# A one-core adaLN block whose 2,121 operations run in a written-out order: another order past the first 140

## The chip, the core and the metric

The kernel runs on one core of a Trainium2 chip. The time is the device time of one execution in microseconds. The core has a matrix engine (TensorE, called PE in the profile; its weight loads are PEld), a vector engine (VectorE, DVE), an activation engine (ScalarE, ACT), a general engine (GpSimd, POOL) and SyncE (SP), which here only issues DMAs. Each engine works off its own instruction list in the order in which the program wrote it, and waits on semaphores that the others raise.

## What is computed

One transformer block with modulation, in bfloat16, on 2048 rows of 640:

```python
mod = (silu(c) @ w_mod).reshape(1, 6, 1, 640)         # sa, ca, ga, sb, cb, gb
h = layernorm(x) * (1 + ca) + sa
q, k, v = split_heads(h @ wqkv)                        # 32 heads of 20
s = q @ k.T * 20 ** -0.5                               # key j is seen by query i if 0 <= i - j < 256
x = x + ga * ((softmax(s) @ v) @ wo)
h = layernorm(x) * (1 + cb) + sb
x = x + gb * ((sigmoid(h @ w_gate) * (h @ w_up)) @ w_down)   # hidden width 1536
```

## The kernel before

**The tiling.** The 2048 rows are cut into eight chunks of 256. A chunk goes through layer norm (`ln1`), the projection to q, k and v (`qkv`), windowed attention (`attention`), the output projection with the residual (`outproj`) and the gated MLP (`mlp`). Chunk a attends to itself and to chunk a-1. All weights stay in SBUF once they are loaded.

**Score groups and bursts.** For each chunk and each half of its heads, attention runs five score groups (three in chunk 0): four "main" ones and one "edge" one, built by `score_set`. All groups write one PSUM tile `S`, which has a single buffer. ACT takes the exponentials out of it into an `E` tile: a main group by one activation of 512 columns and one of 1536, an edge group by four of 512 columns (line 1015). POOL then zeroes what lies outside the window with affine selects (`masks`, line 1040): "far" and "near" over 512 columns, "diag" over 1024. When the four `E` tiles of a half are masked, PE multiplies them by V in one run of matmuls, here called a burst; from chunk 1 on it is issued in front of the second score group of the following half. Each half gives one burst, sixteen in all.

**The other work.** Between score groups PE runs chains of the projections, of `wo` and of the MLP. They write the PSUM tile `M`, which has four buffers; ACT or DVE must empty a buffer before the next chain can use it. ACT applies the tanh from which the sigmoid is made (line 1209), DVE the product with the "up" half (`hh`, line 1211). The gate `gb` is folded into `w_down`: twelve multiplications `wd<-wd,gbc` (line 1192), for which a row `gbc` has to come back from DRAM. The modulation by scale and shift (lines 811 and 812), five column blocks a chunk, and most evacuations of PSUM (lines 893 and 894) may run on ACT, DVE or POOL.

**The order of the work.** `op` records each operation with the engines that can do it. The list `PRIO` (line 342) has one number per recorded operation. `schedule` (line 152) sorts all operations by it; the number modulo 5 names the engine. So `PRIO` fixes each engine's instruction list completely. While it walks through the sorted list, `schedule` also keeps a reckoning of when each operation starts and ends, and uses that for one thing that ends up in the program: where a tile's pool has several buffers, it gives the new tile the buffer that comes free first. `emit` then writes the engines' lists, with a semaphore wait where a producer is on another engine or a buffer has an earlier user. DMAs take 24 semaphores in turn.

Of the kernel before, what the change touches and what calls it, by code (L numbers as in the profile page):

```python
# [25 lines left out]
SWITCH = 0.095  # L26
ENGATTR = {"pe": "tensor", "act": "scalar", "dve": "vector", "pool": "gpsimd", "sp": "sync"}
ENGS = ("pe", "act", "dve", "pool", "sp")
OVERLAP = {"pe": 0.0, "act": 0.085, "dve": 0.075, "pool": 0.045, "sp": 0.0}
# [52 lines left out]
class Prog:  # L82
# [69 lines left out]
    def schedule(self):  # L152


        free = {e: START for e in ENGS}
        bw = 0.0
        lastturn = False
        order = {e: [] for e in ENGS}
        dmacnt = [0] * NDMA
        dmalast = [None] * NDMA  # L160
        rr = 0
        pemode = 0
        portend = 0.0
        freed = {}

        def slot_time(pool, s):
            ten = pool.tenant[s]
            if ten is None:
                if not all(x.done for x in pool.init[s]):
                    return None  # L170
                return max([x.end + x.lat for x in pool.init[s]], default=0.0)
            return None if ten.left else freed[ten]

        def take(t, s):
            ten = t.pool.tenant[s]
            t.prev = list(t.pool.init[s]) if ten is None else list(ten.rel)
            t.slot = s
            t.pool.tenant[s] = t

        for o in sorted(self.ops, key=lambda x: x.prio):  # L180
            assert all(d.done for d in o.deps), o.tag
            e = ENGS[o.prio % 5]
            assert e in o.engs, (o.tag, e)
            o.eng = e
            st = max([o.tmin, free[e] + (SWITCH if e == "pe" and o.mode != pemode else 0.0)]
                     + [d.end + (0.0 if d.eng == "pe" and e == "pe" else d.lat) for d in o.deps])
            if o.isdma and e == "sp":
                st = max(st, bw - QMAX)
            for t in o.tiles:
                if t.slot is None:  # L190
                    step = 1 if t.mate is None else 2
                    best = None
                    for s in range(0, len(t.pool.tenant), step):
                        rts = [slot_time(t.pool, s + k) for k in range(step)]
                        if None not in rts and (best is None or max(rts) < best[0]):
                            best = (max(rts), s)
                    assert best is not None, (o.tag, t.name)
                    if t.mate is None:
                        take(t, best[1])
                    else:  # L200
                        take(t, best[1] + t.odd)
                        take(t.mate, best[1] + 1 - t.odd)
                for x in t.prev:
                    st = max(st, x.end + x.lat)
            if e == "dve" and o.port:
                st = max(st, free["pool"])
            elif e == "pool":
                st = max(st, portend)
            o.start = st
            if e == "pe":  # L210
                pemode = o.mout
            dur = o.dur[e]
            free[e] = st + dur - OVERLAP[e]
            if e == "dve" and o.port:
                portend = free[e]
            if o.isdma:
                turn = o.dlat > 3.0
                if e == "sp" and bw - st > 2.0:
                    free[e] += 0.35 if o.dur[e] > 1.0 else 0.1
                bw = max(st + o.dlat, bw + (MIXED if turn != lastturn and bw > st + o.dlat else 0.0)) + o.work  # L220
                lastturn = turn
                o.end = max(bw - 0.83, st + dur)
                s = rr
                rr = (rr + 1) % NDMA
                dmacnt[s] += 16
                o.key, o.val = f"d{s}", dmacnt[s]
                if dmalast[s] is not None:
                    o.deps.append(dmalast[s])
                dmalast[s] = o
            else:  # L230
                o.end = st + dur
            order[e].append(o)
            o.done = True
            for t in o.tiles:
                t.left -= 1
                if t.left == 0:
                    last = {}
                    for x in t.ops:
                        if x.isdma:
                            last[x] = x  # L240
                    for e2 in ENGS:
                        xs = [x for x in t.ops if x.eng == e2 and not x.isdma]
                        if xs:
                            last[e2] = max(xs, key=lambda x: x.start)
                    t.rel = list(last.values())
                    freed[t] = max(x.end + x.lat for x in t.rel)
        self.order = order
        self.span = max(o.end for o in self.ops)
# [88 lines left out]
def c_pe(n):  # L337
# [3 lines left out]
PE_EPS = 0.14  # L341
PRIO = [
# [124 lines left out]
START = 0.8  # L467
PORTLAG = 0.05
MIXED = 0.55
# [837 lines left out]
```

## Time and profile before

| what | value |
|---|---|
| median of 3 runs | 325.99 us (325.92, 325.99 and one of 528.63) |
| span of the profiled execution, first to last instruction | 324.3 us |
| instructions | 11,594 |
| PE busy | 317.3 us |
| ACT, DVE, POOL busy | 212.3, 211.8, 187.2 us |
| DMA | 37.85 MB |

The execution that was profiled is listed by its span alone; the median of the runs lies 1.7 us above that span. The third run, far above the others, says nothing about the kernel. A busy PE means that at least one matmul was in flight: a matmul of 256 columns is shown with 273 ns, while in a chain the next one starts after 0.109 us.

### The profile page before, as it was taken

The numbers are of one execution on the slowest core, as the hardware profiler recorded it, in microseconds if no ns is written. First come the engines' busy times: TensorE is split into PE (matmuls) and PEld (weight loads), VectorE is DVE, ScalarE is ACT, GpSimd is POOL, SyncE is SP. The second block draws the span as 40 slices with busy tenths as digits, with TensorE's granted clock in tenths as the row PEclk, the third lists the DMA queues.
The fourth block names the chain that finished last, engine by engine and source line by source line (L and its number), as shares of the span: only waits on it lengthen the run. The fifth ranks groups of instructions, "written<-read, shape, count | busy, mean of one in ns | idle before, by whom it ended". The sixth has DMA issues, their size and how long they took to land.

```text
span 324.3 us, 11594 instructions
## 1 busy us (share of the span) xinstructions
PE 317.3 (98%) x4872; PEld 222.7 (69%) x4873; DVE 211.8 (65%) x424; ACT 212.3 (65%) x316; POOL 187.2 (58%) x276
## 2 busy tenths in 40 slices
PE   8999999989999999999999999999999999999997
PEld 3564545446776568765776467877786788787885
DVE  5797898778687959674477475837463769264332
ACT  1899985889876687788687867786767764011120
POOL 5128869976668694847585939382939691012100
DMA  7998799989891383824405394340213032202101
GB/s 249 371 333 299 165 269 180 200 137 183 260 164 22 83 109 77 152 61 101 85 22 82 97 103 110 92 69 5 81 40 88 3 79 53 76 20 64 40 2 40
DMA packets 71694, 37.85 MB, mean 117 GB/s; under 512 B 45274, under 2 KB 70362, under 8 KB 71642
## 3 DMA queue, kind: packets, MB, share of 16 engines
q1 hardware_dynamic: 69616, 35.31, 48.3%
q10 hardware_dynamic: 2026, 1.80, 2.1%
q8 instruction: 38, 0.62, 0.8%
q14 instruction: 14, 0.11, 0.1%
HBM read 21.30 MB, written 5.25 MB: 82 GB/s over the span
## 4 chain that ended last, share of the span: by engine, by line
PE 73%; DMA 2%; SPq 2%; DVE 1%; POOL 1%; issue 0%; DVEq 0%
PE M L668 61%; PE S L669 6%; PE M L669 5%; DMA gbc<-gate 2%; SPq L803 2%; DVE wd L1192 1%; POOL x L793 0%; POOL st L788 0%; DVE hh L1211 0%; POOL E L1040 0%; DVE x L1230 0%; DVEq L310 0%
## 5 line engine op out<-in xcount | busy, mean ns | idle before, releaser
L1040 POOL TENSOR_SCALAR_AFFINE_SELECT E<-E 128x512 bf16<-128x512 bf16 (+1 forms) x176 | 142.6, 836 | 68.7 <-ACT E L1015 67.0
L1015 ACT ACTIVATE E<-S 128x512 bf16<-128x512 f32 (+2 forms) x184 | 150.9, 878 | 47.4 <-PE S L669 46.5
L668 PE MATMUL M<-wqkv,hT 128*128 128x480 bf16 (+1 forms) x340 | 73.9, 355 | 0.6 <-ACT hT L846 0.5
L668 PE MATMUL M<-h2T,wu 128*128 128x256 bf16 x480 | 68.0, 273 | 0.5 <-DVE hh L1211 0.5
L668 PE MATMUL M<-h2T,wg 128*128 128x256 bf16 x480 | 67.8, 273 | 0.0
L668 PE MATMUL M<-wd,hh 128*128 128x320 bf16 (+2 forms) x396 | 58.1, 295 | 0.0
L1209 ACT ACTIVATE sig<-M 128x512 f32<-128x512 f32 x48 | 28.9, 602 | 44.1 <-PE M L668 41.7
L1211 DVE SCALAR_TENSOR_TENSOR hh<-sig,M 128x512 bf16<-128x512 f32 x48 | 32.4, 681 | 37.1 <-ACT sig L1209 24.0
L668 PEld LDWEIGHTS M<-h2T,wu 128*128 128x128 bf16 x480 | 45.9, 98 | 8.4 <-issue 1.2
L668 PEld LDWEIGHTS M<-h2T,wg 128*128 128x128 bf16 x480 | 45.7, 98 | 7.1
L668 PEld LDWEIGHTS M<-wqkv,hT 128*128 128x128 bf16 x340 | 30.1, 98 | 27.6 <-DMA wqkv<-in_A_wqkv_dram 1.6
L668 PEld LDWEIGHTS M<-wd,hh 128*128 128x128 bf16 x396 | 36.8, 98 | 14.3 <-DVE hh L1211 0.2
L669 PEld LDWEIGHTS S<-QT,KT 20*64 20x64 bf16 (+1 forms) x1856 | 19.9, 100 | 21.3 <-ACT E L1015 12.0
L1230 DVE TENSOR_TENSOR x<-M,x 128x320 bf16<-128x320 f32 (+2 forms) x33 | 15.6, 476 | 27.2 <-PE M L668 27.2
L669 PE MATMUL S<-QT,KT 20*64 20x256 bf16 (+5 forms) x1856 | 32.1, 228 | 1.2 <-ACT E L1015 1.2
L776 DVE BATCH_NORM_STATS2 st<-x 128x6 f32<-128x320 bf16 x64 | 28.6, 477 | 2.3 <-DMA x<-in_A_x_dram 1.9
L1082 DVE STREAM_TRANSPOSE T<-M 128x512 f32<-128x512 f32 x32 | 21.5, 698 | 9.2 <-PE S L669 8.0
L668 PE MATMUL M<-wo,oT 128*128 128x320 bf16 x160 | 25.4, 299 | 0.0
L669 PE MATMUL M<-E,V 128*32 128x128 bf16 (+1 forms) x960 | 22.8, 246 | 0.8 <-ACT E L1015 0.4
L781 POOL TENSOR_SCALAR st<-st 128x2 f32<-128x2 f32 x16 | 3.7, 234 | 33.8 <-DVE st L778 33.6
L669 PEld LDWEIGHTS M<-E,V 128*32 128x32 bf16 x960 | 19.2, 97 | 5.3 <-issue 2.9
L1091 DVE STREAM_TRANSPOSE On<-Tn 128x1024 bf16<-128x1024 bf16 x16 | 19.8, 1240 | 0.3
(77 smaller groups left out, 240.2 us busy)
## 6 DMA issues: line engine op xcount, KB each, us to landing
x<-in_A_x_dram SPq DMA_DIRECT2D x23, 160.0 KB, 2.3
doc<-On SPq DMA_DIRECT2D x56, 40.0 KB
wd<-in_B_w_down_dram SPq DMA_DIRECT2D x4, 480.0 KB
wd<-in_w_mod_dram SPq DMA_DIRECT2D x5, 320.0 KB
wqkv<-in_A_wqkv_dram SPq DMA_DIRECT2D x4, 400.0 KB
wu<-in_w_mod_dram SPq DMA_DIRECT2D x5, 320.0 KB
oT<-doc SPq DMA_DIRECT2D x8, 192.0 KB, 2.5
out_dram<-x SPq DMA_DIRECT2D x9, 160.0 KB
```

The lines of the kernel that those rows point to most:

```text
L668: return e.matmul(o, l, r, start=st, stop=sp, skip_group_check=True)
L669: return e.matmul(o, l, r, start=st, stop=sp, tile_position=tp, skip_group_check=True)
L776: A("dve", lambda e, g, bi=bi, j=j: e.bn_stats(v(bi * 12 + j * 6, 6), src[bi].ap[:, j * 320:(j + 1) * 320]), 0.48, reads=[src[bi].r()], wr ...
L781: A("pool", lambda e, g: e.tensor_scalar(v(28, n), var(), EPS, None, op0=ALU.add), 0.2, reads=[st.r(("m", bi)) for bi in range(n)], writes ...
L803: return e.dma_start_transpose(dst(), src())
L1015: A("act", lambda e, eng: e.activation(dst(), src(), ACT.Exp, scale=SM_SCALE), c_act(n), reads=[Sp.r()], writes=[E.r(key)], prio=3, tag=f" ...
L1040: A("pool", lambda e, eng: e.affine_select(rows(dst), rows(src), pattern=[[0, 8], [sign, n]], compare_op=ALU.is_ge, fill=0.0, base=base, c ...
L1082: A("dve", lambda e, g, h=h: e.transpose(T1.ap[:, 512 * h:512 * h + 512], X[h].ap), 0.694, reads=[X[h].r()], writes=[T1.r(h)], prio=3.5, t ...
L1091: A("dve", lambda e, g: e.transpose(On.ap[:], Tn.ap[:]), 1.22, reads=[Tn.r()], writes=[On.r()], prio=4, tag=f"tr2_{a}")
L1209: A("act", lambda e, g, pg=pg, sg=sg: e.activation(sg.ap[:], pg.ap[:], ACT.Tanh, scale=0.5), c_act(512), reads=[pg.r()], writes=[sg.r()], ...
L1211: A("dve", lambda e, g, pu=pu, sg=sg, f0=f0: e.scalar_tensor_tensor(out=hh.ap[:, f0:f0 + 2, :], in0=sg.ap[:].rearrange("p (a b) -> p a b", ...
L1230: A("dve", lambda e, g, ps=ps, bi=bi, c0=c0, n=n: e.tensor_tensor(x1[bi].ap[:, c0:c0 + n], ps.ap[:, 0:n], x1[bi].ap[:, c0:c0 + n], op=ALU. ...
```

## The change

`PRIO` gets other numbers. The first 140 operations in the sorted order stay the same operations in the same order. From there on the order is another, found by a search over draws of whole traces that began at an order with few priced moves. `schedule` no longer keeps its reckoning of time: the buffer of each tile is read from a new list `SLOTS` (709 tiles, numbered in order of first mention), and the constants of the reckoning go. 72 operations change engine:

| operation | moves |
|---|---|
| emptying PSUM of q, k, v (`evqk`, `evv`, `evqt`) | 17 from ACT to DVE, 13 from DVE to ACT |
| transposed x out of PSUM (`ahTe`) | 3 from DVE to ACT, 1 from ACT to DVE |
| modulation ahead of attention (`amodu`) | 3 POOL to ACT, 3 DVE to ACT, 2 ACT to DVE, 2 ACT to POOL |
| modulation ahead of the MLP (`bmodu`) | 7 POOL to ACT, 6 ACT to POOL, 5 DVE to ACT, 3 DVE to POOL, 2 ACT to DVE, 2 POOL to DVE |
| scaling `w_down` (`wds`) | 2 POOL to DVE, 1 DVE to POOL |

ACT then has 337 operations instead of 333, DVE 422 instead of 424, POOL 262 instead of 264; PE keeps 907 and SP 193. The arithmetic of every operation stays as it is.

```diff
-SWITCH = 0.095
-OVERLAP = {"pe": 0.0, "act": 0.085, "dve": 0.075, "pool": 0.045, "sp": 0.0}
...
     def schedule(self):
-        free = {e: START for e in ENGS}
...
+        tiles = {}
+        def number(t):
+            if t is not None and t not in tiles:
+                tiles[t] = len(tiles)
+                number(t.mate)
+        for o in self.ops:
+            for t in o.tiles:
+                number(t)
         for o in sorted(self.ops, key=lambda x: x.prio):
             e = ENGS[o.prio % 5]
             o.eng = e
-            st = max([o.tmin, free[e] + (SWITCH if e == "pe" and o.mode != pemode else 0.0)]
-                     + [d.end + (0.0 if d.eng == "pe" and e == "pe" else d.lat) for d in o.deps])
...
             for t in o.tiles:
                 if t.slot is None:
-                    best = None
-                    for s in range(0, len(t.pool.tenant), step):
-                        rts = [slot_time(t.pool, s + k) for k in range(step)]
...
+                    s = SLOTS[tiles[t]] if SLOTS else 0
+                    ten = t.pool.tenant[s]
+                    t.prev = list(t.pool.init[s]) if ten is None else list(ten.rel)
+                    t.slot = s
+                    t.pool.tenant[s] = t
...
 PRIO = [
-    23, 28, 258, 8, 43, 33, 958, 18, 1448, 38, 3, 507, 513, 72, 67, 48, 53, 58, 76, 84, 101, 99, 144, 149, 154, 159,
+    23, 28, 258, 8, 43, 33, 708, 18, 728, 38, 3, 507, 513, 72, 67, 48, 53, 58, 76, 84, 101, 99, 144, 149, 154, 159,
...
+SLOTS = [
+    0, 1, 3, 2, 0, 0, 0, 1, 0, 2, 0, 1, 3, 0, 1, 2, 3, 0, 0, 1, 0, 2, 0, 0, 3, 1, 0, 4, 5, 1, 3, 2, 2, 3, 2, 1, 3,
...
```

More of the change, by code (lines that the diff above doesn't have):

```diff
@@ L152, in schedule @@
     def schedule(self):
-        free = {e: START for e in ENGS}
-        bw = 0.0
-        lastturn = False
         order = {e: [] for e in ENGS}
@@ L161, in schedule @@
         rr = 0
[L162 to L178, printed above, removed]
+        tiles = {}
[6 more added lines that the diff above has]
+                number(t)
         for o in sorted(self.ops, key=lambda x: x.prio):
@@ L184, in schedule @@
             o.eng = e
-            st = max([o.tmin, free[e] + (SWITCH if e == "pe" and o.mode != pemode else 0.0)]
-                     + [d.end + (0.0 if d.eng == "pe" and e == "pe" else d.lat) for d in o.deps])
-            if o.isdma and e == "sp":
-                st = max(st, bw - QMAX)
             for t in o.tiles:
                 if t.slot is None:
-                    step = 1 if t.mate is None else 2
-                    best = None
-                    for s in range(0, len(t.pool.tenant), step):
-                        rts = [slot_time(t.pool, s + k) for k in range(step)]
[L195 to L215, printed above, removed]
-            if o.isdma:
[L217 to L223, printed above, removed]
-                rr = (rr + 1) % NDMA
[L225 to L231, printed above, removed]
+                    s = SLOTS[tiles[t]] if SLOTS else 0
@@ new lines, in schedule @@
+                    ten = t.pool.tenant[s]
+                    assert ten is not None or all(x.done for x in t.pool.init[s]), (o.tag, t.name)
+                    assert ten is None or ten.left == 0, (o.tag, t.name)
+                    t.prev = list(t.pool.init[s]) if ten is None else list(ten.rel)
+                    t.slot = s
+                    t.pool.tenant[s] = t
+            if o.isdma:
+                dmacnt[rr] += 16
+                o.key, o.val = f"d{rr}", dmacnt[rr]
+                if dmalast[rr] is not None:
+                    o.deps.append(dmalast[rr])
+                dmalast[rr] = o
+                rr = (rr + 1) % NDMA
@@ L237, in schedule @@
                     last = {}
[L238 to L244, printed above, removed]
+                    for x in sorted(t.ops, key=lambda x: x.prio):
+                        last[x if x.isdma else x.eng] = x
                     t.rel = list(last.values())
-                    freed[t] = max(x.end + x.lat for x in t.rel)
         self.order = order
-        self.span = max(o.end for o in self.ops)
     def emit(self):
@@ L338, in c_pe @@
     return max(n, 64) / 2400.0 + 0.0027
-PE_EPS = 0.14
 PRIO = [
[3 rows of a table removed]
[3 rows of a table added]
     92, 87, 187, 237, 242, 247, 253, 263, 272, 267, 280, 275, 290, 300, 305, 286, 317, 296, 322, 311, 376, 357, 386,
[1 row of a table removed]
[1 row of a table added]
     541, 495, 501, 665, 677, 480, 485, 491, 565, 570, 576, 545, 551, 630, 652, 525, 555, 561, 625, 660, 681, 685,
[111 rows of a table removed]
[111 rows of a table added]
+]
+SLOTS = [
[20 rows of a table added]
 ]
@@ L466 @@
 DSAFE = 1.5
-START = 0.8
-PORTLAG = 0.05
-MIXED = 0.55
 NPB = 0
@@ L484 @@
 WSE = (("dve", "pool"), ("dve", "pool"))
-QMAX = 4.5
 WDT = 72.0
```

247 rows, old and new, of tables (PRIO, SLOTS) are left out of this document.

## The prediction

> **What bounds the kernel now.** First the page's busy table, then the table by stage, which says where PE, the busiest engine, still waits.
>
> ```profile
> span 324.3 us, 11594 instructions
> PE 317.3 (98%) x4872; PEld 222.7 (69%) x4873; DVE 211.8 (65%) x424; ACT 212.3 (65%) x316; POOL 187.2 (58%) x276
> ...
> 0.00:12.00 12.00, 9.98 (x88) 5.07 (x90) 7.11 (x24) 4.38 (x10) 4.73 (x25) 1.00 0.86 286
> 12.00:55.00 43.00, 42.46 (x568) 23.54 (x569) 37.31 (x85) 37.08 (x62) 28.26 (x43) 1.00 0.94 261
> 55.00:70.00 15.00, 13.85 (x247) 7.38 (x239) 11.38 (x27) 12.13 (x18) 13.27 (x20) 1.00 1.06 186
> 70.00:90.00 20.00, 19.07 (x353) 14.10 (x356) 15.66 (x28) 16.88 (x28) 13.03 (x17) 1.00 0.93 212
> 90.00:150.00 60.00, 60.00 (x1029) 41.32 (x1018) 46.02 (x92) 43.59 (x62) 41.75 (x56) 1.00 0.51 92
> 150.00:210.00 60.00, 59.99 (x1088) 42.16 (x1087) 36.31 (x68) 46.02 (x67) 40.43 (x56) 1.00 0.47 87
> 210.00:270.00 60.00, 60.00 (x1081) 46.23 (x1079) 34.24 (x62) 43.70 (x61) 42.08 (x57) 1.00 0.24 54
> 270.00:324.30 54.30, 51.91 (x450) 42.88 (x446) 23.74 (x45) 8.47 (x15) 3.65 (x7) 1.00 0.14 40
> ```
>
> The columns are the stretch and its length, then busy time for PE, PEld, DVE, ACT and POOL, then granted clock and DMA. Length less PE busy is PE's idle time: 2.02 us to 12 us, then 0.54, 1.15 and 0.93 us up to 90 us, 0.01 us in the 180 us from 90 to 270, and 2.39 us at the end, where PE is done and the last rows go out. **PE bounds the kernel**, and after 90 us nothing keeps it waiting. The timeline of PE shows what is behind the idle time from 12 to 90 us.
>
> ```profile
> 38.23 0.84 PE L669 MATMUL M<-E,V 128*32 128x256 bf16 x32 [0.35 <-DVE hT L858]
> ...
> 48.66 0.43 PE L669 MATMUL S<-QT,KT 20*64 20x256 bf16 x24 [0.17 <-ACT E L1015]
> ...
> 61.60 0.43 PE L669 MATMUL S<-QT,KT 20*64 20x256 bf16 x24 [0.27 <-ACT E L1015]
> ...
> 64.13 0.43 PE L669 MATMUL S<-QT,KT 20*64 20x256 bf16 x24 [0.30 <-ACT E L1015]
> ...
> 67.91 0.43 PE L669 MATMUL S<-QT,KT 20*64 20x256 bf16 x24 [0.42 <-ACT E L1015]
> ...
> 70.48 1.50 PE L669 MATMUL M<-E,V 128*32 128x128 bf16 x64 [0.42 <-ACT E L1015]
> ...
> 86.54 1.25 PE L668 MATMUL M<-h2T,wu 128*128 128x256 bf16 x10 [0.51 <-DVE hh L1211]
> ...
> 295.58 6.68 PE L668 MATMUL M<-wd,hh 128*128 128x320 bf16 x48
> ```
>
> Seven waits make 2.44 of the 2.62 us. A busy PE isn't always PE at its peak: 48 matmuls of 320 columns in 6.68 us are some 0.136 us from start to start, but one is in flight for 0.30 us, so up to 0.16 us of each wait hides behind the matmul before it. Seven waits hide at most 1.1 us. What an order of the same work can still win is therefore about 2.62 + 1.1 = 3.7 us: it **cannot reach 322 us**. By 2%, about what a measurement of this kernel can tell from no change, faster means under 319.5 us.
>
> **The change part by part.** PE's 907 operations are the same, with the same columns: nothing is added to the bound. I followed the two lists through the recorded operations. SP's 193 DMAs keep their order exactly. PE keeps 624 of its 907 operations in a common order, ACT 226, DVE 258, POOL 156. The sum goes stage by stage, against the span of 324.3 us; the 1.7 us between it and the median of 325.99 are carried over.
>
> *Up to 12 us*: the first 140 operations stand as they were, 0 (±0.2).
>
> *12 to 55 us*: 0.54 us is idle. In front of the second burst ACT now has 48 operations instead of 51, three evacuations of PSUM fewer (one takes 0.58 us in the timeline of ACT below). The rows for what is weighed here and further on:
>
> ```profile
> L1015 ACT ACTIVATE E<-S 128x1536 bf16<-128x1536 f32 x56 | 81.1, 1449 | 17.5 <-PE S L669 17.3
> L1015 ACT ACTIVATE E<-S 128x512 bf16<-128x512 f32 x120 | 67.3, 602 | 29.4 <-PE S L669 29.0
> L811 ACT ACTIVATE hT<-hT,mA 128x256 bf16<-128x256 bf16 x14 | 7.8, 595 | 0.0
> L858 DVE TENSOR_SCALAR hT<-M,mA 128x256 bf16<-128x256 f32 x9 | 4.6, 537 | 0.1
> ```
>
> But the burst at 38.23 us waits for a DVE evacuation of 537 ns into whose `M` buffer it writes; in the new list a transpose and both buffers of the burst still follow such evacuations after 0.4 to 0.6 us of matmuls; those of the burst's own buffers have gone to ACT. The wait stays. I take -0.1, from -0.5 (all idle gone) to +0.5 (the wait twice).
>
> *55 to 70 us*: here ACT decides. Its timeline:
>
> ```profile
> 62.14 1.94 ACT L1015 ACTIVATE E<-S 128x512 bf16<-128x512 f32 x2 [0.59 <-PE S L669]
> 63.97 2.07 ACT L811 ACTIVATE hT<-hT,mA 128x256 bf16<-128x256 bf16 x4
> 65.93 1.92 ACT L1015 ACTIVATE E<-S 128x1536 bf16<-128x1536 f32 x2
> 67.74 0.58 ACT L893 ACTIVATE stg<-M 128x480 bf16<-128x480 f32 x1
> 68.44 1.94 ACT L1015 ACTIVATE E<-S 128x1536 bf16<-128x1536 f32 x2
> ```
>
> `S` has one buffer, so a score group waits for the exponentials of the one before. Four modulations stand together between two groups' exponentials: the group at 64.13 us is written by about 64.5, its exponentials begin only at 65.93, and the group at 67.91 waits for their end. The new list puts two of these modulations there and two one group later. A pair takes about 1.1 us, of which the writing of the group (0.43 us) and its two hand-overs cover the most. So the first pair saves up to 1.0 us at the first place and costs a few tenths at the second. Of 0.42 + 0.42 us at 67.91 and 70.48 I take half back: -0.4, from -0.8 to +0.4. POOL, busy for 13.27 of 15 us here, has the same total of work ahead of the burst at 70.48 in both lists, ACT 0.3 us more; hence the upper end.
>
> *70 to 90 us*: the wait of 0.51 us at 86.54 comes from DVE.
>
> ```profile
> 80.35 0.69 DVE L1211 SCALAR_TENSOR_TENSOR hh<-sig,M 128x512 bf16<-128x512 f32 x1 [0.94 <-ACT sig L1209]
> 83.16 2.65 DVE L1192 TENSOR_TENSOR wd<-wd,gbc 128x640 bf16<-128x640 bf16 x4 [2.12 <-DMA gbc<-gate]
> 85.72 1.27 DVE L1211 SCALAR_TENSOR_TENSOR hh<-sig,M 128x512 bf16<-128x512 f32 x2
> ...
> 73.62 4.26 SPq L803 DMA_TRANSPOSE KT<-stg  x1
> 77.92 0.58 SPq L570 DMA_DIRECT2D gbc<-gate  x1
> ```
>
> DVE stood 2.12 us at a `wd` multiplication whose `gbc` had not landed, and two finished halves of the MLP queued behind it with their `M` buffers full. `gbc` is issued at the same place of SP's list as before, so it lands no earlier. But the new DVE list has three `hh` operations ahead of the first `wd` multiplication instead of one, and then `wd` multiplications by ones, twos and fours between the others. The two `hh` that queued now go first. I take -0.5, from -0.7 to 0; what is late next is the fourth `hh`, behind three multiplications of some 0.55 us, by which time `gbc` is there.
>
> *90 to 270 us*: nothing can be won, so every difference costs. Three things feed PE here.
>
> ```profile
> L1040 POOL TENSOR_SCALAR_AFFINE_SELECT E<-E 128x512 bf16<-128x512 bf16 x112 | 75.8, 689 | 42.5 <-ACT E L1015 42.1
> L1040 POOL TENSOR_SCALAR_AFFINE_SELECT E<-E 128x1024 bf16<-128x1024 bf16 x64 | 69.3, 1093 | 26.2 <-ACT E L1015 24.9
> L1209 ACT ACTIVATE sig<-M 128x512 f32<-128x512 f32 x48 | 28.9, 602 | 44.1 <-PE M L668 41.7
> ```
>
> First the four `M` buffers. Of 290 reuses, 59 had under 1.3 us of matmuls between the last write of the old contents and the first of the new; now 79 have. The price of a tight one: at 38.23 us, 0.38 us of matmuls against an evacuation of 0.537 us cost 0.35 us, so the hand-over adds 0.19 us. A tanh then needs 0.602 + 0.19 = 0.79 us. Two reuses behind a tanh now have 0.70 us and lose 0.1 each; reuses of 0.68 us or more behind a residual (some 0.48 us on DVE) fit. But the engine must also be free at once, and there are 20 more places where it has to be. Second the masks: by the new order POOL has up to 1.5 us less and at most 0.2 us more ahead of the bursts after 130 us, so those come no later. Third ACT: by the eighth burst it has 2.7 us more ahead of it, but in 90 to 150 us ACT is busy for 43.59 of 60 us, so 16 us are free. I take +0.5, from 0 to +3.0 (each of the 20 new tight places losing 0.15 us).
>
> *From 270 us*: the last burst is followed by the same 182 operations of PE in both lists, ending with the same down-projection: 0, to +0.5.
>
> Sum: 0 - 0.1 - 0.4 - 0.5 + 0.5 + 0 = **-0.5 us**; span 323.8, time 325.5 us. The ends add up to -2.2 and +4.6.
>
> **The rivals.** *All waits go.* If stalls between 12 and 90 us vanish with their hidden part and nothing new comes, the time is 325.99 - 3.7 = 322.3, or 323 with a few tenths left. For it: both causes at 67.91 and 86.54 are taken apart. Against it: the wait at 38.23 is still in the list, and the buffers are tighter.
>
> *Buffers and masks come late, by little each time.* If the 20 tighter reuses lose 0.15 us each and the changed ACT order lets three or four bursts start 0.3 us later, +3.0 + 1.0 against the gains of 1.0 gives 329.0. For it: the 0.01 us idle in 180 us shows how exactly the old order fits the chip. Against it: ACT and POOL have a quarter of their time free there.
>
> *Slower by over 2%: a chunk's keys come late and PE cools.* One transposing DMA held SP for 4.26 us (73.62). SP's list is unchanged, but what it transposes is now written by operations that have moved. If one such hold is no longer covered, the score groups behind it, and all work that hangs on them, leave PE idle for 4.3 us. What a long pause then costs shows at the start:
>
> ```profile
> 1.31 2.74 PE L649 MATMUL S<-E 128*128 128x512 bf16 x6 [1.31 <-DVE E L644]
> ...
> 4.33 1.91 PE L649 MATMUL S<-E 128*128 128x512 bf16 x4
> ```
>
> Four matmuls of 512 columns take 1.91 us, the last 0.63 in flight, so some 0.43 us apart, where 0.136 x 512/320 = 0.22 would be full speed. This lasts from 1.31 to about 6 us and loses 2.4 us. Together with the gains not made: 326.0 + 4.3 + 2.4 = 332.7. It decides where a pause gets as long as that, and the longest after 12 us is 0.51 us now: little speaks for it. The Trainium skill, "TensorE: Matmul & The Clock Gate", Part 1, says that the array falls to half its clock after an idle window of about 3.4 us and needs about as much sustained work to come back; by that rule this rival's price is right and the other cases pay none of it. The slow matmuls at the start agree, although the clock column says 1.00 there; no trace here shows a pause of that length later.
>
> *The change does nothing that matters*: PE is bound from 90 us on, and if ACT's and DVE's regrouping is swallowed too, the time stays at 326.0.
>
> **How the numbers follow.** The forecast, 325.5, with its neighbourhood from 324.4 to 327.5 that also holds the last rival: 0.55. All waits go, 322.2 to 324.4: 0.22. Late by little, 327.5 to 332.5: 0.16. Over 332.5: 0.06. Under 319.5, against the bound: 0.01. So faster 0.01, slower 0.06, the same 0.93. The range goes from 323.0, which leaves about 0.08 below, to 329.5, which leaves 0.12 above.
>
> **What would show it.** Right: PE's idle time at 55 to 70 us under 1 us, none behind `hh` near 86 us, modulations on ACT in twos near 64 us, and 90 to 270 us idle for a few tenths. Wrong: PE idle behind tanh, residual or transposed evacuations after 90 us adding to over 2 us; bursts waiting for affine selects; or any PE pause over 2 us.

## The result and the profile after

The changed kernel takes **327.89 us** (median of six runs, 327.73 to 328.31) against 326.06 us for the kernel before beside it (five runs from 325.26 to 326.23, and the one of 528.63): a ratio of 1.0065, with a 95% interval from 1.0054 to 1.0076. By 2% that is no change, and the predicted range of 323.0 to 329.5 us holds it. But the forecast was half a microsecond faster, and the kernel is slower, by 1.8 us in the medians and 2.1 us by the ratio. The span of the profiled execution went from 324.3 to 326.2 us.

The head of the page and the table by stage of the changed kernel; the columns are those of the prediction, with the stretch from 90 us on cut at 110:

```profile
span 326.2 us, 11574 instructions
PE 316.9 (97%) x4872; PEld 221.8 (68%) x4873; DVE 211.8 (65%) x422; ACT 215.1 (66%) x320; POOL 184.8 (57%) x274
```

```profile
0.00:12.00 12.00, 8.96 (x83) 4.21 (x85) 6.70 (x23) 4.06 (x10) 4.71 (x25) 1.00 0.86 278
12.00:55.00 43.00, 42.19 (x561) 23.62 (x560) 39.10 (x89) 35.91 (x59) 27.33 (x43) 1.00 0.92 259
55.00:70.00 15.00, 13.97 (x249) 7.47 (x247) 8.99 (x21) 12.73 (x21) 13.12 (x19) 1.00 1.11 186
70.00:90.00 20.00, 19.16 (x331) 13.65 (x332) 16.05 (x28) 15.57 (x24) 15.13 (x21) 1.00 0.88 213
90.00:110.00 20.00, 18.87 (x332) 13.12 (x323) 18.44 (x38) 12.75 (x19) 12.04 (x17) 1.00 0.51 82
110.00:150.00 40.00, 40.00 (x722) 27.81 (x715) 26.73 (x49) 33.52 (x51) 26.49 (x37) 1.00 0.48 93
...
270.00:326.20 56.20, 53.76 (x515) 44.06 (x512) 24.39 (x45) 10.89 (x19) 3.38 (x7) 1.00 0.16 42
```

PE is busy for as long as before (316.9 against 317.3 us): the work is the same, the idle time grew. By stage, length less PE busy, before and after: to 12 us 2.02 and 3.04; 12 to 55 us 0.54 and 0.81; 55 to 70 us 1.15 and 1.03; 70 to 90 us 0.93 and 0.84; **90 to 110 us 0.00 and 1.13**; at the end 2.39 and 2.44; between 110 and 270 us 0.01 us at most in either. The first of these, up to 12 us, is put down to the execution and not to the change: the first 140 operations are the same, and what PE waits for there is weights from DRAM (0.52 and 0.56 us after, 0.19 us before). Executions of either kernel and of the experiments below have between 2.00 and 3.04 us there (the five built on the old order 2.24 on average, the seven built on the new one 2.56, and the two groups overlap); whether some of the 0.3 us between the averages belongs to the order is not settled. So idle time is compared from 12 to 110 us: **2.62 us before, 3.81 after**.

The waits of PE in the timeline of the changed kernel:

```profile
38.72 0.84 PE L635 MATMUL M<-E,V 128*32 128x256 bf16 x32 [0.17 <-POOL hT L778]
...
53.21 0.43 PE L635 MATMUL S<-QT,KT 20*64 20x256 bf16 x24 [0.52 <-ACT E L981]
...
64.92 0.43 PE L635 MATMUL S<-QT,KT 20*64 20x256 bf16 x24 [0.37 <-ACT E L981]
...
65.89 2.85 PE L634 MATMUL M<-wqkv,hT 128*128 128x480 bf16 x12 [0.55 <-ACT hT L777]
...
71.26 1.50 PE L635 MATMUL M<-E,V 128*32 128x128 bf16 x64 [0.42 <-ACT E L981]
...
89.52 1.50 PE L635 MATMUL M<-E,V 128*32 128x128 bf16 x64 [0.42 <-DVE hh L1177]
...
98.84 0.85 PE L634 MATMUL M<-wo,oT 128*128 128x320 bf16 x5 [1.13 <-DVE x L1130]
```

The new one is the last: the output projection needs an `M` buffer that DVE's residual addition has yet to empty. What DVE did ahead of it, from the timeline of DVE, and POOL's list over the same time:

```profile
86.54 1.76 DVE L1158 TENSOR_TENSOR wd<-wd,gbc 128x640 bf16<-128x640 bf16 x2
...
89.30 2.97 DVE L1158 TENSOR_TENSOR wd<-wd,gbc 128x640 bf16<-128x640 bf16 x4
...
95.71 1.38 DVE L1158 TENSOR_TENSOR wd<-wd,gbc 128x640 bf16<-128x640 bf16 x1
...
97.02 1.37 DVE L1158 TENSOR_TENSOR wd<-wd,gbc 128x640 bf16<-128x640 bf16 x1
...
98.31 1.07 DVE L1130 TENSOR_TENSOR x<-M,x 128x320 bf16<-128x320 f32 x2
```

```profile
95.35 1.40 POOL L1006 TENSOR_SCALAR_AFFINE_SELECT E<-E 128x1024 bf16<-128x1024 bf16 x1 [2.53 <-ACT E L981]
...
96.70 1.34 POOL L1006 TENSOR_SCALAR_AFFINE_SELECT E<-E 128x1024 bf16<-128x1024 bf16 x1
```

The two `wd` multiplications at 95.71 and 97.02 us last 1.38 and 1.37 us. The same instruction, over all ten of before and all eleven of after (shortest, median, longest, in ns):

```profile
L1192 DVE TENSOR_TENSOR wd<-wd,gbc x10: 468/484/866, 83.2 to 93.9; 128x640 bf16<-128x640 bf16 x10
```

```profile
L1158 DVE TENSOR_TENSOR wd<-wd,gbc x11: 430/491/1641, 86.5 to 97.0; 128x640 bf16<-128x640 bf16 x11
```

Its usual time is 0.48 us. The two multiplications in front of the residual additions both start while a POOL select runs, and both end a third of a microsecond after that select: 95.71 + 1.38 = 97.09 against 95.35 + 1.40 = 96.75, and 97.02 + 1.37 = 98.39 against 96.70 + 1.34 = 98.04. The selects are long too: 1.40 and 1.34 us, where the page of before has a mean of 1.093. The residual additions queue behind the two multiplications on DVE, and PE behind them. In the kernel before it is DVE that waits for PE here:

```profile
95.71 1.02 DVE L1164 TENSOR_TENSOR x<-M,x 128x320 bf16<-128x320 f32 x2 [0.56 <-PE M L668]
```

This gave the theory of the **collision**: DVE's multiplication and POOL's instruction can't run at once, whichever comes second stands until the first is done, and the new order puts two multiplications of `wd`, then two residual additions for which PE is short of a buffer, beside two selects.

### The profile page after: what moved, and what is told of

It reads as the page before. It is cut to its first block, busy times and chain, and to the rows that moved or that the text cites. A ratio compares the mean times of both kernels' runs of the same rounds, so it can differ in the third digit from the quotient of the medians.

```text
span 326.2 us, 11574 instructions
## 1 busy us (share of the span) xinstructions
PE 316.9 (97%) x4872; PEld 221.8 (68%) x4873; DVE 211.8 (65%) x422; ACT 215.1 (66%) x320; POOL 184.8 (57%) x274
## 4 chain that ended last, share of the span: by engine, by line
PE 73%; DVE 4%; issue 1%; DVEq 0%
PE M L634 62%; PE S L635 6%; PE M L635 5%; DVE wd L1158 2%; DVE hh L1177 0%; DVE T L1048 0%; DVE x L1130 0%; DVE x L1196 0%; DVE Dr L1053 0%; DVE st L744 0%; DVE Tn L1055 0%; DVEq L259 0%
## 5 line engine op out<-in xcount | busy, mean ns | idle before, releaser
L634 PE MATMUL M<-wqkv,hT 128*128 128x480 bf16 (+1 forms) x340 | 72.2, 355 | 1.1 <-ACT hT L777 0.5
L634 PE MATMUL M<-h2T,wu 128*128 128x256 bf16 x480 | 70.6, 273 | 0.0
L634 PEld LDWEIGHTS M<-h2T,wu 128*128 128x128 bf16 x480 | 45.1, 98 | 7.7 <-issue 0.6
L1130 DVE TENSOR_TENSOR x<-M,x 128x320 bf16<-128x320 f32 x32 | 15.4, 485 | 8.9 <-PE M L634 8.3
```

The costliest lines, as they stand in the source:

```text
L634: return e.matmul(o, l, r, start=st, stop=sp, skip_group_check=True)
L1130: A("dve", lambda e, g, ps=ps, bi=bi, half=half: e.tensor_tensor(x1[bi].ap[:, half * 320:half * 320 + 320], ps.ap[:, 0:320], x1[bi].ap[:, ...
```

## The experiments

Every list below is that of one engine, in the program's tile names, around the place of the edit. Idle time means PE's from 12 to 110 us, from the table by stage of that run; the ratio is to the kernel before on the same chip.

**The changed kernel again, and the order of before in the new code.** The second has the lists `PRIO` and `SLOTS` of the kernel before, so only the way of reading the buffers is new.

> The changed kernel as it is, for a second trace. Theory 'landing': the first 12 us (PE busy 8.96 us instead of 9.98, first score group at 16.19 instead of 15.55 us) were late because the first weights landed late in that one execution; then the first score group of another trace lies anywhere between 15.5 and 16.2 us and the time stays within 327.7 to 328.3 us by other causes. Rival 'program': something in the new program delays the start, and the first score group lies at 16.1 to 16.3 us again. Either way the PE wait of 1.1 us behind the residual add near 98.8 us and the long multiplications of w_down (over 0.9 us) should be there again.

> The order, engines and buffers of the kernel before, written into the new code as lists. Only the code that makes the lists differs. All theories: the time of before within 0.3%, 326.0 us, PE idle 0.5 us near 86.5 us behind the gated product. Theory 'landing': first score group between 15.5 and 16.2 us. Rival 'program': at 15.5 to 15.6 us as in before.

The repeat gave 327.65 us, ratio 1.0053 (1.0036 to 1.0071), idle 4.33 us. Its first score group came at 15.63 us, where the first trace of the changed kernel had 16.19 and that of before 15.55: the late start was that execution's, and not the program's. PE's timeline has two long waits:

```profile
87.33 1.27 PE L634 MATMUL M<-h2T,wu 128*128 128x256 bf16 x10 [1.08 <-DMA wu<-in_B_w_up_dram]
...
98.91 0.85 PE L634 MATMUL M<-wo,oT 128*128 128x320 bf16 x5 [1.10 <-DVE x L1130]
```

The one at 98.9 us is there in both executions; the one for `wu`, whose landing varies, took the place of the one at 89.5 us. The old order in the new code gave 325.64 us, ratio 1.0004 (0.9992 to 1.0015), idle 2.03 us. So the loss is in the order and not in the new code. That run also had no wait at 86 us: 0.37 us idle from 70 to 90 us against 0.93 in the execution that the prediction read. SP issued `gbc` at 76.4 us there, behind a transposing DMA of 3.07 us, against 77.92 us behind one of 4.26: of two executions with the same order, the one in which `gbc` came later has the wait. All theories had expected it again, and so missed this.

**The two multiplications behind the residual additions.** The changed kernel with one edit in DVE's list:

```diff
 T<-M, wd, Dr<-T, wd, Tn<-T,Dr,
-wd, wd, x<-M,x, x<-M,x,
+x<-M,x, x<-M,x, wd, wd,
 hh
```

> The changed kernel with the last two multiplications of w_down on DVE moved behind the two residual adds that follow them. Theory 'lock': these two (1.38 and 1.37 us instead of 0.48) are held by POOL's selects and delay the residual adds, for which PE waits 1.13 us; now that wait is gone, the time is 326.6 to 326.9 us (1.0 to 1.3 us under the changed kernel), ratio to before about 1.002. Rival 'tight buffers': the new order is short of free M buffers all over this stretch, PE waits at the next one instead, and the time stays at 327.5 to 328.0 us.

326.70 us, ratio 1.0024 (1.0014 to 1.0034), idle 3.06 us: 0.9 to 1.3 us of the loss went. DVE's timeline, then PE's:

```profile
96.18 0.49 DVE L1123 TENSOR_TENSOR x<-M,x 128x320 bf16<-128x320 f32 x1 [0.59 <-PE M L627]
96.86 0.49 DVE L1123 TENSOR_TENSOR x<-M,x 128x320 bf16<-128x320 f32 x1 [0.19 <-PE M L627]
97.27 1.06 DVE L1151 TENSOR_TENSOR wd<-wd,gbc 128x640 bf16<-128x640 bf16 x2
```

```profile
98.39 1.80 PE L627 MATMUL M<-wd,hh 128*128 128x320 bf16 x12 [0.20 <-DVE wd L1151]
```

This is what the theory expected, and the rival's time did not come. The two multiplications now take 1.06 us together instead of 2.67, PE no longer waits for the residual, and 0.20 us is left behind `wd` itself.

**The multiplications cut to a tenth.** The changed kernel, with DVE's multiplications over 64 of 640 columns:

```diff
-e.tensor_tensor(wd[:, t, :], wd[:, t, :], gbc[:], op=ALU.mult)
+e.tensor_tensor(wd[:, t, :n], wd[:, t, :n], gbc[:, :n], op=ALU.mult)   # n = 64 on DVE, 640 on POOL
```

> The changed kernel, with the multiplications of `w_down` that DVE does cut to 64 of their 640 columns (POOL's one stays whole). It leaves out most of the scaling by the gate, so its output and its total time aren't those of the block; only the durations of single instructions count. Theory 'the port is held whole': a DVE multiplication that starts while a POOL select or POOL's own multiplication runs still lasts until that POOL instruction ends, whatever its own size: single durations from 0.3 up to 1.6 us, at odds with 0.1 to 0.2 us for the ones that stand alone. Rival 'bandwidth is shared': each is slowed in proportion, the colliding ones last 0.2 to 0.4 us and end at no particular time.

Of DVE's eleven, nine take 0.13 to 0.19 us. The two others, and the selects of POOL beside them:

```profile
86.57 0.61 DVE L1153 TENSOR_TENSOR wd<-wd,gbc 128x64 bf16<-128x64 bf16 x1
...
87.11 0.69 DVE L1153 TENSOR_TENSOR wd<-wd,gbc 128x64 bf16<-128x64 bf16 x1
```

```profile
86.49 0.66 POOL L999 TENSOR_SCALAR_AFFINE_SELECT E<-E 128x512 bf16<-128x512 bf16 x1
...
87.10 0.66 POOL L999 TENSOR_SCALAR_AFFINE_SELECT E<-E 128x512 bf16<-128x512 bf16 x1
```

They end at 87.18 and 87.80 us, the selects at 87.15 and 87.76: 0.03 and 0.04 us after them. For 640 columns it was 0.34 and 0.35, ten times as much for ten times the columns. So a colliding multiplication does nearly all of its work after POOL's instruction has ended; shared in proportion, 64 columns would not have taken 0.6 us. The wait is a lock. The other traces bear it out: in the eleven traces with full multiplications, the 37 that start while a POOL instruction has at least 0.1 us to go all end 0.33 to 0.35 us after it and take 0.62 to 1.69 us; the other 79 take 0.42 to 0.50 us. The Trainium skill, "SBUF — State Buffer", section "SBUF: two separate sides", says this of the pair of ports that VectorE and GpSimd share: an exclusive lock and not a split of bandwidth, which concerns VectorE where it reads two operands from SBUF (or runs in a two-port mode) while GpSimd reads SBUF. Both instructions here are of that kind, and these rows agree. With the cheap multiplications PE has no wait from 90 to 110 us, 2.49 us idle from 12 to 110, and the one timed run is at 326.17 us beside 325.88 for before. That time belongs to a kernel with less work for DVE, whose output is not the block's; what the run shows is the durations.

**The multiplications spread otherwise.** The changed kernel; two fewer ahead of the `hh` for which PE waited at 89.5 us, three behind the first residual additions:

```diff
-wd, wd, st, wd, hh, wd, wd, wd, wd, T<-M, hh, T<-M, wd, Dr, wd, Tn, wd, wd, x, x, hh
+wd, st, hh, wd, wd, wd, wd, T<-M, hh, T<-M, wd, wd, Dr, wd, Tn, x, x, wd, wd, wd, hh
```

> The changed kernel, its twelve multiplications on the same engines, spread otherwise over DVE's list: two fewer ahead of the gated product for which PE waited 0.42 us at 89.5 us, and three instead of none behind the first two residual additions, for which PE waited 1.13 us at 98.8 us. Theory 'the collisions with POOL are nearly the whole loss': both waits go under 0.3 us and the time is 326.0 to 326.6 us against about 325.9 for the kernel before. Rival 'the loss is spread over the whole new order': the waits go and 327 us or more stay.

**Missed**: 327.43 us, ratio 1.0051 (1.0037 to 1.0064), idle 3.48 us. The wait at 89.5 us went and that for the residual too, but PE, DVE and POOL show:

```profile
99.35 1.80 PE L627 MATMUL M<-wd,hh 128*128 128x320 bf16 x12 [1.08 <-DVE wd L1151]
```

```profile
96.26 0.49 DVE L1123 TENSOR_TENSOR x<-M,x 128x320 bf16<-128x320 f32 x1 [0.24 <-PE M L627]
...
97.35 1.94 DVE L1151 TENSOR_TENSOR wd<-wd,gbc 128x640 bf16<-128x640 bf16 x3
```

```profile
95.22 1.76 POOL L999 TENSOR_SCALAR_AFFINE_SELECT E<-E 128x1024 bf16<-128x1024 bf16 x1 [2.53 <-ACT E L974]
```

POOL's first select was held up by DVE (1.76 us), the next ran until 98 us, and the first of the three multiplications with it (1.01 us); now the down-projection waits for the scaled `w_down`. The rival's words, "the waits go and 327 us or more stay", fit this result as well; since the edit made a new collision, the run doesn't decide how much of the loss hangs on collisions.

These rows also show which instruction is spared: the residual addition at 96.26 us, one of whose operands lies in PSUM, takes its usual 0.49 us in the middle of that select. None of the 32 at this line takes longer in either kernel, whatever POOL does. But two operands from SBUF are not the only way to be caught: the normalisation `x<-x,st`, which reads one tensor from SBUF and writes it back there, usually takes 0.44 us and beside POOL up to 0.79 us in the changed kernel.

**All twelve multiplications back between their old neighbours**, in the changed kernel: four in a row on DVE behind the first `hh`, and two of the twelve on POOL.

> The changed kernel with all twelve multiplications of w_down back on the engines and between the same DVE and POOL operations as before; everything else stays changed. Theory 'lock': both waits that the new places made (1.1 us at 98.8 for the residual adds, 0.4 us at 89.5 for a gated product behind multiplications of 0.9 us) go, and the time is 326.0 to 326.4 us, 1.4 to 1.8 us under the changed kernel and within 0.4 us of before. Rival 'the order as a whole': only what moving the last two gave comes back, 326.6 to 327.0 us.

**Missed**: 327.08 us, ratio 1.0045 (1.0028 to 1.0063), idle 4.14 us. Nothing is idle from 90 to 110 us, as expected, but DVE, POOL and PE show a new loss:

```profile
82.97 4.47 DVE L1151 TENSOR_TENSOR wd<-wd,gbc 128x640 bf16<-128x640 bf16 x4 [0.74 <-DMA gbc<-gate]
```

```profile
81.95 6.61 POOL L999 TENSOR_SCALAR_AFFINE_SELECT E<-E 128x512 bf16<-128x512 bf16 x7 [0.87 <-ACT E L974]
```

```profile
88.58 1.25 PE L627 MATMUL M<-h2T,wu 128*128 128x256 bf16 x10 [1.80 <-DVE hh L1170]
```

Four in a row at this place took 2.65 us before (two of them long), where POOL's run of selects was four long, from 84.49 us; here seven run from 81.95 us, and all four collide. So a place in DVE's list is not good or bad by itself: it depends on **what POOL runs at that time**, and POOL's list has moved against it.

**The old order with only these multiplications moved**, to the neighbours that they have in the changed kernel:

> The kernel before with nothing but the twelve multiplications of w_down placed as in the changed kernel (engines too). Theory 'lock': several of them run into POOL's selects, take 0.9 to 1.7 us instead of 0.48, and PE waits behind the residual adds for 0.6 to 1.4 us; time 326.5 to 327.3 us. Rival: the multiplications harm only together with the rest of the new order; time 325.6 to 326.0 us.

**Missed** in time and place, though the collisions came: 327.67 us, ratio 1.0064 (1.0045 to 1.0083), idle 4.08 us. Of three multiplications two collide, one with a select (0.86 us) and one with POOL's own multiplication (1.68 us), and PE waits for the `hh` behind them, not for a residual.

```profile
90.86 2.00 PE L628 MATMUL M<-E,V 128*32 128x128 bf16 x64 [2.06 <-DVE hh L1170]
```

The execution that was profiled is the slowest of six (329.46 us; the others 327.18 to 327.94). So moving these twelve alone, with everything else as before, costs as much as the whole change, at another place.

**Two of the four modulations moved behind both exponentials**, in the kernel before: what the prediction thought that the change did on ACT.

```diff
-hT, hT, hT, hT, E<-S, E<-S, stg<-M
+hT, hT, E<-S, E<-S, hT, hT, stg<-M
```

> The kernel before with two of the four modulations that stand ahead of a score group's exponentials moved behind both of them, which is what the prediction counted on. The prediction's step: 0.4 us faster, 325.4 us, the wait of 0.4 us at 67.9 us shrinks. Rival 'the wait only moves': the projection of chunk 4, due right after that group, needs all modulated columns, so PE waits there instead, 0.5 to 2 us longer; time 326.2 to 327.8 us.

328.60 us, ratio 1.0078 (1.0064 to 1.0093), idle 3.26 us. The rival's mechanism holds; the time is above its range, as a stretch at half clock follows the pause (last section). The score group no longer waits, but the next chunk's projection needs the two modulations:

```profile
68.46 2.58 PE L627 MATMUL M<-wqkv,hT 128*128 128x480 bf16 x6 [1.87 <-ACT hT L770]
```

**The two `hh` ahead of the multiplications that wait for `gbc`**, in the kernel before: `wd, wd, wd, wd, hh` becomes `wd, wd, hh, wd, wd`.

> The kernel before with the second gated product on DVE moved ahead of the third and fourth multiplication of w_down: the one wait after 80 us that the prediction counted as a gain. Prediction's step: 0.5 us faster, 325.4 us. Rival 'only in some executions': that wait exists only where the gate's row lands late (issued at 77.9 us in the trace of before, at 76.4 us in another trace of the same order, which shows no wait); the mean gain is 0 to 0.3 us, 325.6 to 325.9 us, not to be told from before.

325.67 us, ratio 1.0003 (0.9991 to 1.0015), idle 2.03 us, the same as the old order alone. The median gains nothing. In the trace DVE waited 0.72 us for `gbc`, not 2.12 us, so this execution doesn't show what the move is worth when `gbc` comes late.

**The four DMA issues on ACT behind the next group's exponentials**, in the changed kernel, against the wait of 0.52 us at 53.21 us. There ACT's list holds them ahead of the exponentials for which the score group waits:

```profile
48.91 2.21 ACTq L536 DMA_DIRECT2D doc<-On  x4
51.22 1.94 ACT L981 ACTIVATE E<-S 128x512 bf16<-128x512 f32 x2 [2.11 <-PE M L634]
```

> The changed kernel with four DMA issues of ACT (the attention output of chunk 0 to DRAM) moved behind the exponentials of the score group that follows them. Theory 'head of line': these issues wait for DVE's transpose, the exponentials queue behind them (begun at 51.22 us for a group written by 49.9), and PE waits 0.52 us at 53.21; without it that wait goes and the time falls by 0.3 to 0.6 us to about 327.4 us. Rival: ACT is late there for other work, or the gain is given back at the groups from 64 to 71 us; the time stays within 0.2 us of 327.9.

327.35 us, ratio 1.0047 (1.0033 to 1.0060), idle 4.55 us. The time is the 327.4 us that the theory named, and 0.3 us under the repeat of the changed kernel; but the intervals of the two ratios overlap, and the execution that was profiled took 328.76 us, the other four 327.25 to 327.43. In that execution the score group doesn't wait, and the projection behind it does, as the evacuation of `V` stands behind the four issues:

```profile
54.49 2.20 PE L627 MATMUL M<-wqkv,hT 128*128 128x480 bf16 x10 [1.26 <-ACT V L852]
```

The four wait for DVE's transposed output; in this trace moving them moved the wait, and what the move is worth in the other executions stays open. None of these versions is faster than the kernel before.

## Why the prediction was wrong

**What held.** PE bounds the kernel and no order comes under 322 us: all versions lie between 325.6 and 328.6 us. After 110 us PE has no wait in any of them, so the forecast's largest worry, the 20 tighter reuses of `M` (0 to +3.0 us), cost nothing there; tanh, residual and masks kept up. The last stage is +0.05 us, where 0 was said. The rival with the late keys did not come, and of the rival by which buffers and masks come late by little each time, one late buffer showed after 90 us, at 98.84 us, and it was late by 1.13 us.

**90 to 270 us, +0.5: the step that failed.** 1.13 us was lost, inside the bounds, at one place and for a reason that none of its three terms has; that the total fell inside the bounds is luck. The path is that of the first term, a buffer of `M` behind a residual addition. But it was not a tight reuse: by PE's timeline at least 1.3 us of matmuls lie between the last write of the old contents and the point where PE stood, twice the 0.68 us that the step reckoned enough. What failed is the condition that "the engine must also be free at once", which got no price of its own: DVE was held by two multiplications that met POOL's selects and took 1.38 and 1.37 us where 0.48 is usual. Whether DVE's operations meet POOL's instructions was not among the "three things". The price of a `wd` multiplication was taken, one stage earlier, as "some 0.55 us", the mean of a group that ran from 0.468 to 0.866 us; up to 1.64 was measured. The spread was in the trace before, and so was the rule in the code: the reckoning that the change removes kept DVE's marked operations and POOL's apart.

```python
if e == "dve" and o.port:
    st = max(st, free["pool"])
elif e == "pool":
    st = max(st, portend)
```

The prediction read these lines as bookkeeping whose one product was the buffer of a tile. They also stated which operations exclude each other. The changed program still carries the marks (`port=True`), but nothing uses them. With the rule, the two engines' new lists would have had to be laid against each other in time, above all for the twelve multiplications, both of whose operands lie in SBUF.

**70 to 90 us, -0.5.** Two faults. The 0.51 us at 86.54 us was a wait of one execution: with the same order it was gone when `gbc` was issued earlier, and the move that should undo it gained nothing in the median (1.0003). "It lands no earlier" took the place in SP's list for the time: the issue lay at 77.92, 76.37 and, in the changed kernel, 76.35 us. And the first two multiplications that now stand between the `hh` met POOL's selects (1.76 us together), so that the `hh` behind them was late and PE lost 0.42 us at 89.52 instead; a third, at 89.30 us behind that `hh`, took 1.64 us. Measured -0.09 against that execution, +0.47 against the other one of the old order.

**55 to 70 us, -0.4.** The list was misread: "two there and two one group later". The trace shows all four ahead of the same group's last exponential:

```profile
64.75 1.08 ACT L777 ACTIVATE hT<-hT,mA 128x256 bf16<-128x256 bf16 x2
65.73 0.59 ACT L981 ACTIVATE E<-S 128x512 bf16<-128x512 f32 x1
66.21 1.09 ACT L777 ACTIVATE hT<-hT,mA 128x256 bf16<-128x256 bf16 x2
67.19 1.44 ACT L981 ACTIVATE E<-S 128x1536 bf16<-128x1536 f32 x1
```

`S` comes free no sooner than before. The wait of 0.42 us for the group went, and 0.55 us for the modulated columns came; the stage won 0.12 us. And had the list been as it was read, the loss would have been 2.9 us by the experiment (328.60 against 325.70: the wait of 1.87 us and matmuls at half clock behind it), far outside the +0.4 of that step: it priced the group that waits for ACT and not the projection that waits for the moved pair.

**12 to 55 us, -0.1.** Measured +0.27, inside its bounds. The wait at 38 us shrank from 0.35 to 0.17 us, and a new one of 0.52 came behind ACT's four DMA issues, which stand behind the second burst, where the step weighed nothing.

**Up to 12 us, 0 (±0.2).** Between the two profiled executions this stage is +1.02 us, five times its bounds. The average of all traces of either order differs by 0.3 us, so most of it is this pair of executions, in which the first weights landed at different times.

**The sum.** Stage by stage the two profiled executions differ by +1.02, +0.27, -0.12, -0.09, +1.13 and +0.05 us, where the forecast had 0, -0.1, -0.4, -0.5, +0.5 and 0: the two gains were not made, and the loss was twice as large. The two executions in the new order that were profiled have 3.81 and 4.33 us idle from 12 to 110 us, the two in the old order 2.62 and 2.03: 1.75 us apart, and the ratios 1.0053 and 1.0065 say 1.7 to 2.1. Of it, 0.9 to 1.3 us hang on the two multiplications at 95.7 us, which is shown by moving them. That a lock against POOL is what makes them long is shown by the short ones. The remaining 0.8 us is shared by the wait at 53 us, `hh` at 89.5 us, what is left at 98 us and the first weights; it isn't settled how, since the attempts to take more of it away met the lock again. The prediction took 2% for about what a measurement of this kernel can tell; the intervals here reach 0.1 to 0.2% to each side. Its counts of operations in common order are a little low (637 for PE, 232 for ACT, 268 for DVE and 163 for POOL by the two lists, instead of 624, 226, 258 and 156); no term rests on them.

## What to carry to other kernels

A duration from a group's mean hides that an instruction is fast alone and slow beside another engine: look at the shortest and the longest, and at what POOL runs under each long one. When lists of DVE and POOL move against each other, lay the operations of DVE that the lock catches (here those that read two operands from SBUF, and some from SBUF to SBUF with one) against POOL's in time, and price each meeting at the rest of POOL's instruction plus most of its own time, here 0.34 of 0.48 us. A wait seen in one execution behind a DMA may be that execution's alone; look at a second execution before counting on it.

## What the hardware showed that was not expected

In two experiments a PE pause of about 2 us was followed by matmuls at half speed. The table by microsecond for PE alone (stretch, length, PE busy, granted clock, DMA share, GB/s), first of the old order with the moved multiplications, then of the one with the moved modulations:

```profile
91.00:92.00 1.00, 1.00 (x49) 0.86 1.22 175
92.00:93.00 1.00, 1.00 (x32) 0.50 1.50 156
...
94.00:95.00 1.00, 1.00 (x6) 0.50 2.50 191
95.00:96.00 1.00, 1.00 (x11) 0.94 0.12 18
```

```profile
68.00:69.00 1.00, 0.54 (x2) 0.74 0.05 5
69.00:70.00 1.00, 1.00 (x4) 0.50 0.90 187
70.00:71.00 1.00, 1.00 (x11) 0.50 1.11 225
71.00:72.00 1.00, 1.00 (x27) 0.55 0.52 103
```

Adding up by how much each microsecond's clock falls short of 1: (0.14 + 0.50 + 0.50 + 0.50 + 0.06) / 0.5 = 3.4 us at half clock in the first (93 to 94 us is at 0.50 as well), and (0.26 + 0.50 + 0.50 + 0.45) / 0.5 = 3.4 us in the second, so up to 1.7 us each on top of the pauses of 2.06 and 1.87 us. In the profiled executions the pause of 1.80 us in the changed kernel with its multiplications moved back, and all shorter ones after 12 us, left the clock at 1.00. In the first experiment only the profiled execution of six had a lowered mean clock (0.995), and how long the others paused isn't known; in the second all four had.

The Trainium skill, "TensorE: Matmul & The Clock Gate", Part 1, states the halved clock and a window of about 3.4 us, and the 3.4 us at half clock agree with it. It puts the fall after an idle window of that length; here pauses of 1.87 and 2.06 us were enough, and the measurement decides. That the windows run freely, as the page has it, would let one pause be punished and another of nearly the same length not; in both cases the 3.4 us ahead of the fall were some 40% busy by the timeline (1.3 and 1.4 us), but no run here varied this, so where the threshold lies stays open. For the prediction's rival with the late keys it means that it needs no pause of 4 us: 1.9 us was enough here, and its price was the pause plus up to 1.7 us, where the prediction read 2.4 us from the start of the kernel.
